# One load instead of two for w3, two instead of three for wq's side columns, and x in parts: a decode step on one core

## The chip, the cores and the metric

The kernel runs on one core of a Trainium2 chip. The metric is device time in microseconds (us), the median over several runs. A ratio in this document is the mean time of one kernel's fast runs over that of the other's fast runs of the same rounds, so it is not quite the ratio of the medians that stand beside it. Its 95% interval is about plus or minus 0.13%, that is 0.2 us: effects below that are not resolved by the times.

## The reference

Four sequences decode one token each: layer norm, attention with a cached window, a residual, layer norm, a gated MLP, a residual.

```python
# x (4,1,1024); wq (1024,4096); wo (4096,1024); w1, w3 (1024,3584); w2 (3584,1024); all bf16
W = min(4096, max(256, Sk // 4))                    # 2048 cached positions of 4 KV heads x 128
q = layernorm(x) @ wq                               # 32 query heads x 128
o = softmax(q @ k[:, :, Sk-W:].T * Dh**-0.5) @ v[:, :, Sk-W:]
h = x + o @ wo
n = layernorm(h)
out = h + (silu(n @ w1) * (n @ w3)) @ w2
```

Every weight and every cached key and value is used once. 55.6 MB have to come from HBM, and the arithmetic on them is small.

## The kernel before

All large loads go through one SBUF ring of 160 KiB a partition and are issued by SyncE (SP) in the order of a plan. A load that overwrites ring space waits until the matmuls that read that space are done.

```python
CE = 512
SETS = [(0, 5, 4), (80, 3, 2), (104, 3, 2)]     # "side" loads: 128 rows of wq, last 512 columns each
...
plan = [                                         # ring place, source, row width, first row, rows
    ("wq", load_rows, (0, wq_v, N_Q, 0, 4)),
    ("side", load_side, SETS[0]), ("side", load_side, SETS[1]), ("side", load_side, SETS[2]),
    ("wq", load_tail, (32 * KIB, wq_v, N_Q, 4, 4)),   # without those 512 columns of its last row
    ("k", ...), ("k", ...), ("v", ...), ("v", ...),    # each two DMAs of 2 MiB
    ("wo", load_rows, (32 * KIB, wo_v, D, 0, 32)),
    ("w1", load_rows, (96 * KIB, w1_v, N_F, 0, 8)),
    ("w3", load_rows, (0, w3_v, N_F, 0, 4)),
    ("w3", load_rows, (28 * KIB, w3_v, N_F, 4, 4)),
    ("w2", ...), ("w2", ...), ("w2", ...), ("w2", ...),
]
...
nc.scalar.dma_start(out=x_sb[:], in_=x_flat)     # x for the first norm, issued by ScalarE (ACT)
load_next(8)
...
nc.scalar.dma_start(out=x_q[0:P:RS, :], in_=...) # x for the residual, issued by ACT
...
for i in range(IO):                              # o @ wo
    ...
    if i == 11:
        load_next()                              # w3's second half lies where wo's rows 0 to 11 lay
load_next()
...
gate_up("w1", g_ps); ...; gate_up("w3", u_ps)    # 64 matmuls each
```

The "side" loads take 1 KB of wq from each of 128 partitions' rows and bring it in on a few partitions. In the packet records at most seven of these packets run at a time, so they use a few DMA engines only. The bulk load, whose 128 packets are spread evenly over all 16 engines, gets 8 KB an engine shorter.

Completion of DMAs is told by eight semaphores, used in turn. The built program makes a DMA wait until the one eight places before it (SP's and ACT's together) has landed.

## Time and profile before

| | before |
|---|---|
| median time | 138.03 us (137.86 to 138.07, 6 runs) |
| span in the profile | 136.1 us |
| bulk DMA queue, share of 16 engines' span | 95.6% |
| TensorE (PE) busy | 54% |

From the page of the kernel before: busy tenths of 40 equal slices of the span for PE and for the DMA engines, then GB/s in these slices, then the DMA queues (packets, MB, share of 16 engines' span).

```profile
PE   0202980979898989810535906793096440900960
DMA  5999999999999999999979999989899999989970
GB/s 156 463 464 404 404 438 405 424 428 438 433 428 419 429 443 428 429 522 477 462 327 443 481 409 404 477 371 477 354 430 426 438 455 442 430 389 419 421 288 5
...
q1 hardware_dynamic: 2731, 55.58, 95.6%
q8 instruction: 8, 0.13, 0.3%
...
q14 instruction: 2, 0.02, 0.0%
```

PE has slices of 0, the DMA engines have none between the first slice and the last. Two queues carry the engines' instructions.

The chain of waits of the kernel before, its last part (start us, us, what):

```profile
75.97 22.91 DMA ring<-in_B_w_dram
98.88 0.04 issue
98.92 2.41 PE g_ps L455 x17
101.34 0.07 SPq L93
101.41 0.05 issue
101.46 31.31 DMA ring<-in_B_w_dram
132.77 0.04 issue
132.81 0.32 PE y_ps L485 x4
133.13 0.02 issue
133.15 0.37 ACT res L495
```

The last DMA was issued at 101.46 and landed 31.31 us later. That is not how long 256 KB take: it is the queue ahead of it. After the landing come four matmuls and a copy, then the store.

The timeline of the kernel before (start us, us, engine, line, operation, count; in brackets the idle time before and what ended it), rows of the first norm, the first q matmuls, the up-projection and the down-projection:

```profile
4.55 0.54 DVE L183 TENSOR_SCALAR xn<-x_sb,mv,rstd 4x1024 bf16<-4x1024 bf16 x1
...
12.86 3.58 PE L259 MATMUL q_ps<-ring,xnT 128*4 128x512 bf16 x32 [6.78 <-DMA ring<-in_A_wq_dram]
...
107.38 3.18 PE L455 MATMUL u_ps<-ring,hnT 128*32 128x448 bf16 x32 [2.94 <-DMA ring<-in_B_w_dram]
...
115.83 3.18 PE L455 MATMUL u_ps<-ring,hnT 128*32 128x448 bf16 x32 [5.27 <-DMA ring<-in_B_w_dram]
...
120.18 1.70 DVE L477 STREAM_TRANSPOSE hgT<-hg 128x896 bf16<-128x896 bf16 x1
121.94 0.10 PEld L485 LDWEIGHTS <-hgT 128*32 128x32 bf16 x1 [3.73 <-DVE hgT L477]
126.09 3.82 PE L485 MATMUL y_ps<-ring,hgT 128*32 128x256 bf16 x68 [7.08 <-DMA ring<-in_B_w_dram]
```

Normalised x (`xn`) is there 8 us before the first q matmul, which waits for wq. The down-projection's weights (hgT) are loaded at 121.94, and its first matmul waits until 126.09 for w2. Both are slack in front of a landing.

### The profile page before, as it was taken

The numbers are of one execution on the slowest core, as the hardware profiler recorded it, in microseconds if no ns is written. First come the engines' busy times: TensorE is split into PE (matmuls) and PEld (weight loads), VectorE is DVE, ScalarE is ACT, GpSimd is POOL, SyncE is SP. The second block draws the span as 40 slices with busy tenths as digits, with TensorE's granted clock in tenths as the row PEclk, the third lists the DMA queues.
The fourth block names the chain that finished last, engine by engine and source line by source line (L and its number), as shares of the span: only waits on it lengthen the run. The fifth ranks groups of instructions, "written<-read, shape, count | busy, mean of one in ns | idle before, by whom it ended". The sixth has DMA issues, their size and how long they took to land.

```text
span 136.1 us, 2343 instructions
## 1 busy us (share of the span) xinstructions
PE 73.8 (54%) x1050; PEld 45.0 (33%) x1050; DVE 43.4 (32%) x79; ACT 31.1 (23%) x36; POOL 1.7 (1%) x8
## 2 busy tenths in 40 slices
PE   0202980979898989810535906793096440900960
PEld 0200220267474747400024905571043210300840
DVE  6820000044243434471984001206100695080000
ACT  3000000016555555518385200000002300000001
POOL 5000000000000000000000000000000000000000
PEclk9999999999999999997555555579757777555577
DMA  5999999999999999999979999989899999989970
GB/s 156 463 464 404 404 438 405 424 428 438 433 428 419 429 443 428 429 522 477 462 327 443 481 409 404 477 371 477 354 430 426 438 455 442 430 389 419 421 288 5
DMA packets 2789, 55.75 MB, mean 410 GB/s; under 512 B 311, under 2 KB 471, under 8 KB 731
## 3 DMA queue, kind: packets, MB, share of 16 engines
q1 hardware_dynamic: 2731, 55.58, 95.6%
q8 instruction: 8, 0.13, 0.3%
q10 hardware_dynamic: 48, 0.02, 0.1%
q14 instruction: 2, 0.02, 0.0%
HBM read 55.59 MB, written 0.01 MB: 408 GB/s over the span
## 4 chain that ended last, share of the span: by engine, by line
DMA 54%; PE 24%; ACT 11%; DVE 5%; SPq 2%; issue 1%; ACTq 0%
DMA ring<-in_B_w_dram 40%; DMA ring<-in_A_wq_dram 15%; PE kt_ps L315 10%; ACT kT L321 5%; PE scores_ps L300 5%; ACT z L356 3%; PE q_ps L259 3%; SPq L119 2%; PE g_ps L455 2%; DVE rmax L332 2%; ACT Pm L337 2%; PE OT_ps L378 2%; DVE pT L346 1%; DVE z L352 1%; ACT L337 1%
## 5 line engine op out<-in xcount | busy, mean ns | idle before, releaser
L321 ACT COPY kT<-kt_ps 128x1024 bf16<-128x1024 bf16 x16 | 15.9, 1013 | 13.1 <-PE kt_ps L315 13.1
L315 PE MATMUL kt_ps<-ident,ring 128*128 128x128 bf16 x256 | 17.8, 230 | 0.0
L315 PEld LDWEIGHTS <-ring 128*128 128x128 bf16 x256 | 15.8, 104 | 4.9 <-issue 4.9
L319 DVE COPY kT<-kt_ps 128x1024 bf16<-128x1024 bf16 x16 | 11.1, 692 | 16.2 <-PE kt_ps L315 16.2
L259 PE MATMUL q_ps<-ring,xnT 128*4 128x512 bf16 x63 | 7.2, 626 | 10.5 <-DMA ring<-in_A_wq_dram 10.5
L378 PE MATMUL OT_ps<-z,ring 128*128 128x32 bf16 x256 | 7.5, 188 | 9.0 <-ACT z L356 5.0
L455 PEld LDWEIGHTS <-hnT 128*32 128x32 bf16 x128 | 5.3, 137 | 19.3 <-issue 16.6
L300 PE MATMUL scores_ps<-kT,qz 128*32 128x512 bf16 x64 | 9.9, 610 | 2.9 <-ACT kT L321 2.9
L455 PE MATMUL u_ps<-ring,hnT 128*32 128x448 bf16 x64 | 6.4, 576 | 8.2 <-DMA ring<-in_B_w_dram 8.2
L378 PEld LDWEIGHTS <-ring 128*128 128x128 bf16 x256 | 7.4, 105 | 9.8 <-issue 9.7
L485 PE MATMUL y_ps<-ring,hgT 128*32 128x256 bf16 x112 | 5.8, 375 | 8.3 <-DMA ring<-in_B_w_dram 8.1
L455 PE MATMUL g_ps<-ring,hnT 128*32 128x448 bf16 x64 | 5.5, 529 | 5.2 <-DMA ring<-in_B_w_dram 5.2
L485 PEld LDWEIGHTS <-hgT 128*32 128x32 bf16 x112 | 4.5, 130 | 10.2 <-issue 5.9
L259 PEld LDWEIGHTS <-xnT 128*4 128x4 bf16 x63 | 2.0, 115 | 14.8 <-issue 14.7
L277 DVE TENSOR_SCALAR q_sb<-q_ps 128x512 bf16<-128x512 f32 x1 | 0.7, 692 | 19.5 <-PE q_ps L259 19.5
L495 ACT CAST res<-y_ps 128x256 bf16<-128x256 f32 x1 | 0.4, 372 | 26.4 <-PE y_ps L485 26.4
L356 ACT ACTIVATE z<-pt_ps,mask 128x512 bf16<-128x512 f32 x8 | 5.3, 687 | 3.5 <-DVE z L352 3.5
L348 PE MATMUL pt_ps<-pT,perm 128*128 128x512 bf16 x4 | 2.4, 608 | 6.8 <-DVE pT L346 6.8
L278 ACT ACTIVATE q_sb<-q_ps 128x512 bf16<-128x512 f32 x1 | 0.6, 597 | 23.6 <-DVE q_sb L277 23.6
L405 PE MATMUL y_ps<-ring,o 128*32 128x256 bf16 x128 | 5.5, 352 | 0.8 <-DVE o L394 0.8
L352 DVE TENSOR_SCALAR z<-pt_ps,mask 128x512 bf16<-128x512 f32 x8 | 5.5, 738 | 1.2 <-ACT z L356 0.8
L469 DVE RECIPROCAL eg<-eg 128x896 f32<-128x896 f32 x1 | 5.8, 5754 | 0.0
(79 smaller groups left out, 50.2 us busy)
## 6 DMA issues: line engine op xcount, KB each, us to landing
ring<-in_A_k_cache_dram SPq DMA_DIRECT2D x4, 2048.0 KB, 25.4
ring<-in_A_v_cache_dram SPq DMA_DIRECT2D x4, 2048.0 KB, 39.0
ring<-in_B_w_dram SPq DMA_DIRECT2D x1, 7168.0 KB
ring<-in_B_w_dram SPq DMA_DIRECT2D x2, 3584.0 KB, 23.3
ring<-in_B_w_dram SPq DMA_DIRECT2D x1, 4352.0 KB
ring<-in_A_wq_dram SPq DMA_DIRECT2D x1, 4096.0 KB, 12.1
ring<-in_A_wq_dram SPq DMA_DIRECT2D x1, 3968.0 KB, 19.8
ring<-in_B_w_dram SPq DMA_DIRECT2D x1, 1792.0 KB
```

What stands on the lines that cost most here:

```text
L259: nc.tensor.matmul(q_ps[QD * g : QD * g + B, hf * 512 : hf * 512 + n], lhsT=xnT[:, kc, :], rhs=wq_t[:, c0 : c0 + n], start=(kc == 0), stop ...
L300: nc.tensor.matmul(scores_ps[QD * g : QD * (g + 1), n * 512 : (n + 1) * 512], lhsT=qz_v[:, z0 : z0 + QD], rhs=kT_v[:, g, :, :], start=(b = ...
L315: nc.tensor.transpose(out=kt_ps[:, jj, :], in_=k_v[:, n * NJ + t * TB + jj, :], identity=ident[:])
L319: nc.vector.tensor_copy(out=kT[:, t * TB : (t + 1) * TB, :], in_=kt_ps[:])
L321: nc.scalar.copy(out=kT[:, t * TB : (t + 1) * TB, :], in_=kt_ps[:])
L352: nc.vector.tensor_scalar(out=z[:, :, g, :], in0=pt_ps[:], scalar1=mask[:, g : g + 1], scalar2=None, op0=ALU.mult)
L356: nc.scalar.mul(out=z[:, :, g, :], in_=pt_ps[:], mul=mask[:, g : g + 1])
L378: nc.tensor.matmul(OT_ps[:, b, :], lhsT=loaded["v"][b][:, j, :], rhs=PTz[j // NJ][:, (j % NJ) * B + b, :, :], start=(j == 0), stop=(j == J ...
L405: nc.tensor.matmul(y_ps[QD * j : QD * (j + 1), :], lhsT=o4[:, i, :, :].rearrange("p b s -> p (b s)"), rhs=loaded["wo"][i][:, j * CG : (j + ...
L455: nc.tensor.matmul(out_ps[QD * j : QD * (j + 1), hf, :HF], lhsT=hnT[:, k, :], rhs=loaded[kind][k][:, c0 : c0 + HF], start=(k == 0), stop=( ...
L469: nc.vector.reciprocal(out=eg[:], in_=eg[:])
L485: nc.tensor.matmul(y2_ps[QD * j : QD * (j + 1), :], lhsT=hgT[:, i, :], rhs=loaded["w2"][i][:, j * CG : (j + 1) * CG], start=False, stop=(i ...
```

## The change

Its intent: fewer and larger loads (w3 in one DMA with runs of 56 KiB, the side columns in two DMAs), and x in parts so that its first half can be used early. The DMAs of the program stay 24 in number.

```diff
-    SETS = [(0, 5, 4), (80, 3, 2), (104, 3, 2)]
+    SETS = [(0, 5, 4), (80, 3, 4)]
 ...
-        ("side", load_side, SETS[2]),
 ...
-        ("w3", load_rows, (0, w3_v, N_F, 0, 4)),
-        ("w3", load_rows, (28 * KIB, w3_v, N_F, 4, 4)),
+        ("w3", load_rows, (0, w3_v, N_F, 0, 8)),
 ...
-    nc.scalar.dma_start(out=x_sb[:], in_=x_flat)
-    load_next(8)
+    for c in range(2):
+        nc.scalar.dma_start(out=x_sb[:, c * 512 : (c + 1) * 512], in_=x_flat[:, c * 512 : (c + 1) * 512])
+    load_next(7)
 ...
-    nc.scalar.dma_start(out=x_q[0:P:RS, :], in_=x_flat.rearrange("b (j c) -> j b c", j=JG))
+    for c in range(2):
+        nc.scalar.dma_start(
+            out=x_q[c * 2 * QD : (c + 1) * 2 * QD : RS, :],
+            in_=x_flat.rearrange("b (j c) -> j b c", j=JG)[2 * c : 2 * c + 2],
+        )
 ...
-        if b % BS == BS - 1:
+        if b == 1:
             load_next()
```

The last hunk takes away the place where w3's first half was loaded, behind the last use of v.

## The prediction

> **What bounds the kernel now.** The DMA engines, nearly throughout: the slice table shows DMA 9 in almost all 40 slices, the queue table 95.6% of 16 engines' span for 55.6 MB. Landings, from chain of waits and timeline: w1 98.88 us, w3's halves 107.38 and 115.83, w2's parts 126.09, 130.34, 132.18, 132.81. From w1 to w3's end: 7.34 MB in 16.95 us = 433 GB/s. The Trainium skill, "DMA: Bandwidth & Descriptors", section "Where 436 GB/s comes from", states a ceiling of 435.2 GB/s; this trace agrees. Compute only has to be ready when data lands; after the last landing come 4 matmuls, a 0.37 us copy and the store.
>
> **What the change does.**
>
> 1. *w3 in one DMA, later.* The DMA timeline shows w3's first half issued at 84.0 us, the second at 89.0 (behind wo's row 12), w2 at 91.4. Now all of w3 is issued near 89. The queue does not run dry: w1 was issued at 75.97 and lands at 98.9, so 8 to 10 us of work are still queued. Packet records: a 28,672 B packet takes 1062 ns, a 57,344 B one 2116: 8 ns less a pair, 8 pairs an engine, about 0.07 us saved.
>
> 2. *w3 consumed later.* The first 32 up-projection matmuls no longer start at 107.4; all 64 wait for about 115.7. Two runs of 3.18 us in the timeline give 6.1 us at the half clock: end near 121.9 instead of 119.0; product (1.09) and transpose (1.70) then end near 124.8. w2 lands near 126: 1.2 us of slack left of 4. Off the critical path.
>
> 3. *Side columns in two DMAs.* One SP issue of 0.7 us is spared, but the next wq load is then issued at 3.0 instead of 3.8 us while the first keeps the engines busy until 12.3: nothing. The 128 packets of 1 KB (46 ns) stay, on the same few engines.
>
> 4. *x in parts.* The first matmul waits for wq until 12.83 us. x's second half goes behind wq packets; the x_q packets (one each 1.23 us, between 32 KiB packets) show how slow that is. Estimate: landing at 6 to 8 us, normalised x at 9 to 10.5, still before 12.83. x_q's 27 ns packets move to the two[...] engines: an estimated 0.05 to 0.1 us there.
>
> 5. *Completion semaphores.* Eight, used in turn; the DMAs stay 24. Some k and v issues now wait for other landings (the second k load for wq's first part, 12.8 us instead of 5.0), while 10 us of work are queued. No drain.
>
> **On the critical path:** only engine time, -0.07 us from w3, +0.05 to +0.1 on two engines: about zero.
>
> **Predicted: 137.95 us, 8 in 10 between 137.4 and 138.6.** Faster by over 2%: 0.01; within 2%: 0.97; slower: 0.02.
>
> **What would show it.** Right: DMA 9 throughout, w3 landing at 115.5 to 116, w2's last part at 132.5 to 133; one up-projection wait of about 11 us; the wait for w2 down from 7 us idle to about 1.3. Wrong: a slice near 97 us with DMA below 7; y matmuls waiting for the transposed product instead of w2; first q matmul after 13 us.
>
> **What would make it wrong:** a late x half that delays the q projection; an instruction fetch behind 57 KB packets that stalls TensorE past 126 us; uneven engine loads, since the last landing is that of the slowest engine.

## The result

The changed kernel takes 138.02 us (137.85 to 138.31, 6 runs), the kernel before 138.03 us. The ratio is 1.0005, with a 95% interval of 0.9992 to 1.0018: the same.

From the page of the changed kernel, the same lines, and below them the end of its chain of waits:

```profile
DMA  5999999999999999999979999999989989989960
GB/s 155 463 462 405 423 429 390 452 414 433 433 419 443 419 438 438 409 527 476 462 327 462 462 409 404 493 404 426 438 370 510 455 370 400 470 348 436 426 266 5
...
q1 hardware_dynamic: 2584, 55.58, 95.4%
```

```profile
98.76 2.41 PE g_ps L458 x17
...
101.29 31.45 DMA ring<-in_B_w_dram
...
132.79 0.32 PE y_ps L488 x4
...
133.13 0.37 ACT res L498
```

The same bytes in 147 fewer bulk packets keep the engines as busy as before, and the last w2 part lands at 132.75 instead of 132.77 us.

Where SP issued w3 (timeline of SP's queue), first the two halves in the kernel before, then the one load in the changed kernel:

```profile
84.01 0.33 SPq L93 DMA_DIRECT2D ring<-in_B_w_dram  x1
...
89.01 0.33 SPq L93 DMA_DIRECT2D ring<-in_B_w_dram  x1
```

```profile
88.78 0.33 SPq L93 DMA_DIRECT2D ring<-in_B_w_dram  x1
```

The timeline of the changed kernel, the rows that answer to those of before:

```profile
7.92 0.68 DVE L179 BATCH_NORM_STATS2 stats<-x_sb 4x6 f32<-4x512 bf16 x1 [4.74 <-DMA x_sb<-in_A_x_dram]
9.38 0.53 DVE L186 TENSOR_SCALAR xn<-x_sb,mv,rstd 4x1024 bf16<-4x1024 bf16 x1
...
12.86 3.58 PE L262 MATMUL q_ps<-ring,xnT 128*4 128x512 bf16 x32 [1.95 <-DMA ring<-in_A_wq_dram]
...
90.72 2.15 PE L408 MATMUL y_ps<-ring,o 128*32 128x256 bf16 x72 [1.56 <-issue]
...
115.84 5.49 PE L458 MATMUL u_ps<-ring,hnT 128*32 128x448 bf16 x64 [11.59 <-DMA ring<-in_B_w_dram]
...
122.51 1.70 DVE L480 STREAM_TRANSPOSE hgT<-hg 128x896 bf16<-128x896 bf16 x1
124.26 0.10 PEld L488 LDWEIGHTS <-hgT 128*32 128x32 bf16 x1 [3.37 <-DVE hgT L480]
126.11 3.82 PE L488 MATMUL y_ps<-ring,hgT 128*32 128x256 bf16 x68 [4.78 <-DMA ring<-in_B_w_dram]
```

Much has moved, and none of it moved a landing. x is ready 4.83 us later (9.38 against 4.55), and q still starts at 12.86. All 64 up-projection matmuls now run after 115.84; their result is ready 2.3 us later (weights loaded at 124.26 against 121.94), and w2 still starts at 126.11. PE also stood still for 1.56 us at 89.2, in the middle of wo, a wait for which the profile shows no releaser. It ended 1.5 us after a packet of the instruction queue, so a late instruction block is likely, but no run tests it. It cost nothing either.

### The profile page after: what moved, and what is told of

Its sections match the earlier page's. It is cut to its first block, busy times and chain, and to the rows that moved or that the text cites. A ratio compares the mean times of both kernels' runs of the same rounds, so it can differ in the third digit from the quotient of the medians.

```text
span 136.2 us, 2339 instructions
## 1 busy us (share of the span) xinstructions
PE 72.5 (53%) x1050; PEld 44.9 (33%) x1050; DVE 43.3 (32%) x77; ACT 31.1 (23%) x36; POOL 1.7 (1%) x8
## 4 chain that ended last, share of the span: by engine, by line
DMA 55%; PE 23%; ACT 11%; DVE 5%; SPq 2%; issue 1%; ACTq 0%
DMA ring<-in_B_w_dram 40%; DMA ring<-in_A_wq_dram 15%; PE kt_ps L318 10%; ACT kT L324 5%; PE scores_ps L303 5%; ACT z L359 3%; PE q_ps L262 3%; PE g_ps L458 2%; DVE rmax L335 2%; ACT Pm L340 2%; PE OT_ps L381 2%; DVE pT L349 1%; SPq L119 1%; DVE z L355 1%; ACT L340 1%
## 5 line engine op out<-in xcount | busy, mean ns | idle before, releaser
L458 PE MATMUL u_ps<-ring,hnT 128*32 128x448 bf16 x64 | 5.5, 529 | 11.6 <-DMA ring<-in_B_w_dram 11.6
L193 PE MATMUL tp_ps<-ident,xn 4*128 4x4 bf16 x8 | 0.7, 200 | 10.0 <-DVE xn L186 10.0
L408 PEld LDWEIGHTS <-o 128*32 128x32 bf16 x128 | 4.1, 118 | 4.4 <-DVE o L397 1.9
```

The source lines that it names most:

```text
L408: nc.tensor.matmul(y_ps[QD * j : QD * (j + 1), :], lhsT=o4[:, i, :, :].rearrange("p b s -> p (b s)"), rhs=loaded["wo"][i][:, j * CG : (j + ...
L458: nc.tensor.matmul(out_ps[QD * j : QD * (j + 1), hf, :HF], lhsT=hnT[:, k, :], rhs=loaded[kind][k][:, c0 : c0 + HF], start=(k == 0), stop=( ...
```

## The experiments

The theory to test (A): the DMA engines bound the kernel from the second slice to the last, so what changes neither the engines' work nor lets them run dry changes nothing. The rivals: B, parts of the change gain and lose and cancel; C, a late x costs; and that a chain of compute is the bound.

### Is it bound by bytes? Half of w3

A wrong result: only w3's rows 0 to 3 are loaded, and used twice. All compute stays.

```diff
-        ("w3", load_rows, (0, w3_v, N_F, 0, 8)),
+        ("w3", load_rows, (0, w3_v, N_F, 0, 4)),
-                        rhs=loaded[kind][k][:, c0 : c0 + HF],
+                        rhs=loaded[kind][k % len(loaded[kind])][:, c0 : c0 + HF],
```

> Wrong result on purpose: only rows 0 to 3 of w3 are loaded and used twice; all instructions of compute stay. Theory A: 3.67 MB at 433 GB/s are gone, 8.5 us: 129.5 to 129.9. Rival (a chain of compute bounds the kernel): stays above 135.

Measured: 129.65 us against 137.93, ratio 0.9397 (0.9383 to 0.9411); 8.3 us less for 3.67 MB. The timeline of this run:

```profile
117.30 0.10 PEld L488 LDWEIGHTS <-hgT 128*32 128x32 bf16 x1 [5.72 <-DVE hgT L480]
117.64 3.46 PE L488 MATMUL y_ps<-ring,hgT 128*32 128x256 bf16 x68 [5.61 <-DMA ring<-in_B_w_dram]
```

w2 lands 8.5 us earlier, as the bytes say, and the compute in front of it has 0.34 us of slack left. So bytes are the bound, and the rival of a compute chain falls. It also shows what lies close behind: with some 0.3 us of transfers less, this matmul would wait for compute and not for w2. That need not cost time at once, since PE waits 0.79 us more for w2's next part (121.89 in this run's timeline); no run goes there.

### Each part alone

Each of these is the kernel before with one part of the change.

```diff
 e1: w3 in one load, and "if b == 1" in place of "if b % BS == BS - 1"
 e2: both loads of x in two parts each
 e3: SETS = [(0, 5, 4), (80, 3, 4)], load_next(7), one "side" entry less
```

> Only w3 in one DMA behind wo's row 12. Theory A (the kernel is bound by the DMA engines, each part of the change alone is worth nothing): same as before within 0.2%, at most 0.1 us faster (8 ns saved on each of 8 packet pairs an engine). Theory B (parts that gain and cost cancel): w3 alone is faster by 0.3 us or more, or slower by that much because its first half is issued 5 us later.

> Only x in two parts each. Theory A: same within 0.2%; normalised x about 5 us later than before, the first q matmul still at 12.9 us. Theory B: slower by 0.3 us or more, which w3 or the side columns give back in the whole change.

> Only the side columns in two DMAs instead of three. Theory A: same within 0.2%, the same 128 packets of 1 KB on the same few engines. Theory B: faster by 0.3 us or more, since one issue of 0.7 us on SP is spared.

| run (5 each) | median us | ratio to before | 95% interval |
|---|---|---|---|
| before | 138.02 (9 runs) | | |
| w3 alone | 137.93 | 0.9997 | 0.9984 to 1.0009 |
| x alone | 138.68 | 1.0047 | 1.0035 to 1.0060 |
| side alone | 138.05 | 1.0004 | 0.9990 to 1.0017 |

w3 and the side columns do what theory A says. x alone does not: it costs 0.65 us, and all its runs (138.50 to 138.82) lie above all of the kernel before. The whole change contains it and costs nothing. That looked like theory B, a cancelled cost. But neither of the other parts gains anything alone, so they do not pay for it: together they must take it away. The next runs look for how.

### A late x, and a queue that runs dry

Two ways of making x later still. In the first the first x load comes in four parts. Ten loads then stand before the first k load, and with eight completion semaphores the second wq load has to wait for the landing of the first. In the second, x_q stays in one load, and the second wq load waits only for x's first part, which lands at once.

```diff
 e8: changed kernel, and
-    for c in range(2):
-        nc.scalar.dma_start(out=x_sb[:, c * 512 : (c + 1) * 512], ...)
+    for c in range(4):
+        nc.scalar.dma_start(out=x_sb[:, c * 256 : (c + 1) * 256], ...)
 e10: as e8, and x_q in one load as in the kernel before
```

> The changed kernel with the first x load in four parts. Two things come of it: normalised x near 15.5 us instead of 9.9, and ten loads stand before the first k load, so that with eight completion semaphores the second wq load must wait for the landing of the first. Theory A: the second is worth time: issue at 12.85 instead of 3.0, first packet about 13.9 instead of 12.3, some 1.6 us without packets: 139.3 to 139.9. Rival C (only a late x would cost): see the run with late x alone.

> The first x load in four parts, the second one in one, so that the second wq load stands ninth and waits only for x's first part, which lands early. x is late as in the run with ten loads (first q matmul near 15.5 us instead of 12.86), but the queue stays full. Theory A: the q projection has 10.8 us until the second wq load lands at 23.6 and needs 7.1: 138.0 within 0.3. Rival C (a late x costs): 139 or more.

With four parts and ten loads: 140.65 us, ratio 1.0196 (1.0181 to 1.0211), 2.7 us more, beyond the 1.4 to 2.0 expected. SP's timeline of this run, the issue of the second wq load:

```profile
13.05 0.34 SPq L125 DMA_DIRECT2D ring<-in_A_wq_dram  x1
```

Two windows of one microsecond each of this run (last two columns: mean busy share of the DMA engines and GB/s), then the same windows of the changed kernel:

```profile
12.00:13.00 1.00, 0.00 (x0) 0.00 (x0) 0.06 (x1) 0.00 (x0) 0.00 (x0) 1.00 0.22 74
13.00:14.00 1.00, 0.00 (x0) 0.00 (x0) 0.81 (x2) 0.12 (x1) 0.00 (x0) 1.00 0.19 65
```

```profile
12.00:13.00 1.00, 0.14 (x4) 0.10 (x7) 0.48 (x4) 0.00 (x0) 0.00 (x0) 1.00 1.20 491
13.00:14.00 1.00, 1.00 (x12) 0.28 (x8) 0.00 (x0) 0.00 (x0) 0.00 (x0) 1.00 1.27 535
```

The queue ran dry. By the packet records the second wq load's first packets start at 14.17 us in the mean instead of 12.49, 1.68 us later, as expected. What the expectation missed is that its packets are then slow at first (their times sum to 10.10 us an engine instead of 9.44), and that the chains of packets that ended wq first did so at 24.0 us instead of 21.5, 2.5 us later. So this is the price of an empty queue: the gap and about 0.7 us of starting again. The chains that ended wq last did so only 1.2 us later (24.5 instead of 23.3), because their side packets ran in the gap (all start before 13.94 us); still the last bulk packet of the kernel ends 2.57 us later (134.97 instead of 132.40). This run also has the extra packet that the next section is about, but it fell on a chain that ended w3 at 116.59 us, while the last one did so at 117.93: in this profile it adds nothing.

With late x alone: 138.34 us, ratio 1.0030 (1.0015 to 1.0045), 0.4 us more, where theory A said nothing. The timeline of this run:

```profile
14.24 0.53 DVE L182 TENSOR_SCALAR xn<-x_sb,mv,rstd 4x1024 bf16<-4x1024 bf16 x1
...
15.75 3.58 PE L258 MATMUL q_ps<-ring,xnT 128*4 128x512 bf16 x32
...
19.26 3.57 PE L268 MATMUL q_ps<-t,xsT 20*4 20x512 bf16 x8
...
23.56 3.58 PE L258 MATMUL q_ps<-ring,xnT 128*4 128x512 bf16 x31 [0.73 <-DMA ring<-in_A_wq_dram]
```

q started 2.9 us late, and caught up with 0.73 us to spare before the second wq load landed at 23.56 us. So the late x did not delay q's end. Another cost is in this run, as in x alone.

### What x alone and late x have in common

The packet records (start, duration, queue, size of each packet) answer it. Two 8 KB packets on instruction queue 14 come after 40 us in every run. Start of each in us, end of the last bulk packet in us, and the ScalarE instructions in the built program (each trace has one record fewer, so the differences can be read there too):

```
run                   8 KB packets      last bulk packet   ScalarE instructions
before                60.17   135.57        132.46                68
changed               59.95   134.19        132.40                69
w3 alone              58.84   135.43        132.29                68
side alone            58.42   135.81        132.52                67
x alone               60.47   109.03        132.97                70
late x alone          60.08   108.76        132.69                70
x in four parts       61.25   111.81        134.97                71
```

With 69 instructions or fewer, the second one comes after the last landing, where the DMA engines have nothing to do. With 70 or more it comes near 109 us, in the middle of w3. It follows the 62nd ScalarE record of the trace by 1 to 4 us in the profiled executions (by 5 us in x in four parts): that record is the exponential of the gate at 106.04 us in x alone and the final copy at 133.13 us in the changed kernel. That a block of instructions is full at this count is the likely reading; no run looks into the block. x in parts adds two DMA instructions to ScalarE. Merging two side loads takes one of its semaphore waits away. The whole change is at 69, x alone at 70.

How a packet of 0.31 us can cost more than its own time: bulk packets of one DMA engine follow each other within nanoseconds, so the records can be strung into 16 chains. Ends of w3 on the 16 chains, sorted, us (stringing can swap two chains at a disturbance; the set of ends does not depend on it):

```
changed:  113.69 113.70 113.77 113.78 114.10 114.91 115.04 115.05 115.06 115.08 115.12 115.14 115.22 115.30 115.32 115.36
x alone:  113.56 113.73 113.75 113.86 114.12 114.93 115.07 115.08 115.09 115.11 115.12 115.27 115.30 115.33 115.33 115.93
```

Eleven chains are late and five early. As far as the stringing tells, the late ones carried many side packets (three chains end wq at 23.1 to 23.3 us, most at 21.5 to 22.1) or one of PE's 16 KB instruction blocks, which makes its engine about 1.4 us later (wo's end to w3's end takes 35.23 us on a chain with one, 33.82 us on one without). The other chains keep their 33.82 us, so the others do not make up for what one engine loses. In x alone one chain stands out by 0.6 us: the extra 8 KB made it 0.55 us later, and it was already among the latest. And w3 and each w2 part land when the last engine is done. With x in four parts the same packet fell on a chain that was not among the latest, and w3's last end is not that chain's.

### ScalarE's instruction count by itself

Theory D says that one ScalarE instruction too many is the whole cost. Two runs: the changed kernel with one tiny copy more, and late x with one ScalarE copy moved to VectorE.

```diff
 e11: changed kernel, and
+    idle = act.tile([B, 1], FP32)
+    nc.scalar.copy(out=idle[:], in_=rstd[:])
 e12: e10, and
-    nc.scalar.copy(out=bc[:], in_=bc_ps[:])
+    nc.vector.tensor_copy(out=bc[:], in_=bc_ps[:])
```

> The changed kernel with one more ScalarE instruction, a copy of 4x1 near 9 us, off the path. It tests theory D, formed from the runs so far: x alone cost 0.65 us because ScalarE's program then has one instruction more than a block of its instruction fetch holds; the 8 KB fetch that otherwise comes at 134 us, after the last landing, comes at 109 us on a DMA engine that is already among the last. The built programs count 67 to 69 ScalarE instructions in the runs without that early fetch, 70 and 71 in the three with it; this one has 70. Theory D: an 8 KB packet of the instruction queue near 109 us, last landing near 132.9, 138.4 to 138.7 us. Theory A (only bulk packets count): 138.0.

> The run with late x alone again (four parts of the first x load, 70 ScalarE instructions, 138.34), with one PSUM copy moved from ScalarE to VectorE, so 69 instructions. x stays as late (first q matmul near 15.5 us). Theory D: the fetch goes back to 134 us, 138.0 within 0.2. Rival C (the late x cost the 0.4 us): stays at 138.3 to 138.4.

One more: 138.44 us, ratio 1.0027 (1.0014 to 1.0040). Its 8 KB packet starts at 109.08, the last bulk packet ends at 133.02. One chain ends w3 at 115.98, the next at 115.44; it shows a gap of 0.30 us and a packet 0.25 us longer at 109, together 0.55 us. The landing of w3, for which the up-projection waits, moves with it. It was 115.83 us in the kernel before and 115.84 in the changed one; here is x alone, then one more:

```profile
116.41 3.18 PE L460 MATMUL u_ps<-ring,hnT 128*32 128x448 bf16 x32 [5.81 <-DMA ring<-in_B_w_dram]
```

```profile
116.46 4.57 PE L460 MATMUL u_ps<-ring,hnT 128*32 128x448 bf16 x64 [12.71 <-DMA ring<-in_B_w_dram]
```

Late x with one less: 138.20 us, ratio 1.0013 (1.0001 to 1.0026), packet at 134.14, last bulk packet at 132.41. The last long step in the chains of waits, first x alone, then one more, then late x with one less:

```profile
101.41 31.89 DMA ring<-in_B_w_dram
```

```profile
101.52 31.85 DMA ring<-in_B_w_dram
```

```profile
101.44 31.27 DMA ring<-in_B_w_dram
```

The first of the two shows it: one 4x1 copy, off the path, brings back the early fetch and some 0.4 us. It does not show all 0.65 us of x alone. In the profiles w2's last part lands 0.53 us later in x alone than in the kernel before, and 0.62 us later with one copy more than in the changed kernel. But the latter profile is of the slowest of its five executions (138.64 us, the others 138.27 to 138.48). So 0.4 of the 0.65 us is shown by an added instruction. The rest may be the same packet or another cost of x in parts, and x alone with one ScalarE instruction less was not run.

The second agrees in its profile: x is as late as in late x alone (first q matmul at 15.83), and w2's last part lands at 132.7 again. But this profile is of the fastest of its six executions (138.01 us, the others 138.15 to 138.44). Its mean time lies between the two answers, 0.2 us above the kernel before, and the times do not tell it from late x with 70 (1.0013 against 1.0030). So a small cost of the very late x, or of the moved copy, is not excluded.

### What did not test what it was meant to

Two runs were to find where a later w3 starts to cost, by moving its place in the code behind all of wo, and behind w1's first row.

```diff
 e5: e6:
-        if i == 11:
-            load_next()
-    load_next()
 e5:
+    load_next(2)
 e6, in gate_up:
+            if kind == "w1" and k == 0:
+                load_next(2)
```

> The changed kernel with w3 issued behind the whole of wo (near 92 us) instead of behind its row 12 (88.8). Theory A: w1's packets keep the engines busy until 96.7 to 98.5, so the queue does not run dry: 138.0 within 0.3. Rival (the issue time counts): about 3 us slower, 141.

> The changed kernel with w3 and w2 issued only behind the first row of w1's matmuls, that is after w1 has landed. Theory A: issue near 99.1 us, first packet about 1 us later, near 100.2, while the engines end w1 at 96.7 to 98.5: dry for 1.7 us on the latest engine and 2.5 in the mean, so 139.8 to 140.7 us, a slice near 99 us with DMA 5 or less, and all later landings moved by the same amount. Rival (landing is decided by compute): 138.0.

Measured: 138.07 us (ratio 1.0004, 0.9990 to 1.0019) and 137.99 us (1.0003, 0.9986 to 1.0019). The expectation for the second failed, since w3 was not issued late. SP's timeline of that run, w3 and w2's first part:

```profile
86.60 3.18 SPq L93 DMA_DIRECT2D ring<-in_B_w_dram  x2
```

A load is held back by the reads and writes of the space that it overwrites, and by the loads ahead of it in SP's queue. Its place in the code is no wait. w3 lies over wo's rows 0 to 11, so it goes when row 12 starts, wherever it is written (88.69 in the first of these runs; PE was 2.2 us ahead in the second). So how late w3 may be issued before the engines run dry stays untested; w3 alone shows that the 5 us of its first half are free, and the run with ten loads shows what running dry costs.

### The size of runs, and the side columns

w3 in eight loads of 7 KiB runs at the same place; and the changed kernel with no side columns, where the second wq load brings whole rows.

```diff
 e9:
-        ("w3", load_rows, (0, w3_v, N_F, 0, 8)),
+        *[("w3", load_rows, (r * 7 * KIB, w3_v, N_F, r, 1)) for r in range(8)],
 e4: "side" entries, their transposes and their eight matmuls removed, load_rows in place of load_tail
```

> The changed kernel with w3 in eight DMAs of 7 KiB runs, issued at the same place. Packet times of the traces fit 8 ns plus bytes at 27.2 per ns (28,672 B 1062, 57,344 B 2116, 6,144 B 234), so a 7,168 B packet takes 271 to 272 ns and w3 17.4 us of each engine instead of 16.93. Theory A with that packet cost: about 0.45 us slower, 138.4 to 138.6. Theory A without (packet starts overlap): 138.0.

> The changed kernel without side columns: the second wq load brings all of its 32 KiB rows. If the last landing is that of an engine that has no side packets (one with an instruction fetch), it gets 8 KB more, 0.3 us: 138.3. If the engines with side packets are the last, it gets faster by up to 0.5 us: 137.5. Theory A proper, total engine time only: 0.37 us of 46 ns packets become 0.30 us of bulk, no change.

Eight loads: 138.40 us, ratio 1.0031 (1.0019 to 1.0044), 0.4 us more as expected. So a cost for each packet is real. In the 16 chains it is less than 8 ns, since packets overlap by some 3 ns: undisturbed chains take 34.12 us from wo's end to w3's end with eight loads, 33.86 with two (the kernel before) and 33.82 with one. w3 in one load is worth 0.04 us against two: too little to see in the times. No side columns: 138.18 us, ratio 1.0012 (0.9999 to 1.0024). Having them gains some 0.2 us, at most 0.3, just short of being resolved. So the time does not tell the first of the three expected answers from the third; it excludes the second, a faster kernel.

No run with a right result beats both kernels by more than the noise. What is left is the engines' own work: 55.6 MB.

## Why the prediction was right

The time held. Point by point:

1. *w3 in one load, later.* Right. Alone it is 137.93 us. It saved 0.04 us on an undisturbed chain, not 0.07. Its landing at 115.84 was inside the 115.5 to 116 named. The Trainium skill, "DMA: Bandwidth & Descriptors", section "Where 436 GB/s comes from", gives 435.2 GB/s as the ceiling of the SBUF ports; the trace of the kernel before has 433 from w1's landing to w3's and agrees. The same section says that for transfers from HBM the limit of about 358 GB/s binds; here, with one core at work, it did not.
2. *w3 consumed later.* Right in kind, the slack was larger. The 64 matmuls took 5.49 us, not 6.1, since they do not all run at the half clock (0.50 granted until 120 us, 0.80 from 120 to 121.3). The weights were ready at 124.26 and w2 came 1.85 us later, not 1.2. The wait that it named as a sign, "down from 7 us idle to about 1.3", mixes two measures: PE's idle time in front of w2 fell from 7.08 to 4.78 us, the slack behind the weights from 4.15 to 1.85.
3. *Side columns.* Right, alone 138.05 us.
4. *x in parts.* The mechanism that it named is right: second half used at 7.92 us (6 to 8 said), x normalised at 9.91 (9 to 10.5 said), first q matmul still 12.86. The Trainium skill, "DMA: Bandwidth & Descriptors", section "Queues, rings and completion order", says that an engine takes a packet from each queue in turn; here x_q's packets of 512 B do come one every 1.23 us, one bulk packet of 1.21 us apart, so the trace agrees. But the step "only engine time, +0.05 to +0.1 on two engines" missed the real price of this part: 0.65 us alone, of which 0.4 us is shown to come through ScalarE's instruction count. (x_q's 16 packets do run as two streams of eight, where there were four of four; what that costs was not measured by itself.)
5. *Completion semaphores.* Right for this change: the queue stayed full. In the run with ten loads the same mechanism was worth 2.7 us.

The sum was right, with one term missing. The prediction named uneven engine loads and instruction fetches as risks, but thought of a stalled PE, not of a fetch that takes time on the slowest DMA engine. The change stays free of that by one ScalarE instruction. That is luck: the prediction did not count these instructions. With three side loads beside x in parts, as in the run with x alone, it would have been about 138.7 us, by an estimate from that run: w3 in one load was not in it.

## What to carry to other kernels

In a kernel that keeps the DMA queue full from start to end, moving a load, waiting longer for it or being late with its consumer is free until a landing waits for compute or the queue runs dry; read both margins from the timeline before costing anything else. Where every engine is full, the last landing is that of the most loaded engine, so look at everything that adds to one engine, the instruction blocks of the compute engines too. When a part tested alone costs more than the whole, ask what its companions removed: here a single wait in an instruction stream.

## What the Trainium skill lacked or had wrong

- "Runtime: NRT & Kernel Launch", section "Instruction fetch mechanics", calls the cost of a block boundary "one DMA tail-bump, mostly hidden". Hidden from the sequencer or not, the block takes time on one of the bulk DMA engines: about 1.4 us for each of PE's 16 KB blocks, 0.55 us for ScalarE's 8 KB. One added instruction, which brought the latter forward, cost 0.4 us. No page says so.
- The same section gives blocks of 16 KiB, without a difference between the engines. The eight packets of the queue that fits PE's instruction count are 16,384 B; those of the queue that follows ScalarE's are 8,192 B. Whether these are whole blocks the records do not tell.
- "DMA: Bandwidth & Descriptors", section "Specifications", gives about 27 GiB/s an engine. Packet durations here fit 8 ns plus bytes at 27.2 B per ns, that is 27.2 GB/s or 25.3 GiB/s; 16 times that is 435 GB/s.
- The same page, section "SWDGE vs HWDGE vs iDMA", gives packets of at most 4096 B "preferably" as the boundary where an engine switches, in a table on DMAs issued by GpSimd. It gives no size for loads issued by SP and ACT: here a small packet of another queue waits for a whole run of 32,768 B (1.23 us a turn).
- The same page gives no cost of a queue that runs dry: here a gap of 1.68 us and about 0.7 us of slow packets after it.
